# Loads of keys and values split between two DMA queues, in a one-token attention block

## The chip, the cores and the metric

The kernel runs on one core of a Trainium2 chip. The core has five engines that run their own instruction streams: TensorE (PE, matrix products), VectorE (DVE), ScalarE (ACT), GpSimd (POOL) and SyncE (SP), which here does nothing but issue DMAs. Sixteen DMA engines move data from the device memory into the on-chip memory of 128 partitions. An engine that issues a DMA puts it on its own DMA queue; SP's queue is q1 in the profile, ScalarE's is q10. Engines wait for one another, and for DMAs, on semaphores.

The metric is the device time of one execution in microseconds (us), the median of several runs. All times below are microseconds from the start of the profiled span unless something else is said.

## The reference

One token goes through a transformer block: layer norm, attention against a long cache, a projection with a residual, then a second layer norm and a small dense block. What counts is the attention, with 32 heads, 32,768 cached positions and a head size of 128, in bfloat16:

```
q = (layernorm(x) @ wq)                      # 512 -> 32 heads x 128
scores = einsum("bhqd,bhkd->bhqk", q, k_cache) * (Dh ** -0.5)
p = softmax(scores)
o = einsum("bhqk,bhkd->bhqd", p, v_cache)
h = x + o @ wo
out = h + (act(layernorm(h) @ w1 + b1)) @ w2     # 512 -> 1376 -> 512
```

The keys of one head are 32,768 x 128 x 2 bytes = 8.39 MB, and so are its values. Over 32 heads that makes 537 MB to read for one token; the weights add some 11 MB. Each byte is used once.

## The kernel before, in words

**Loads.** One head's keys (or values) are loaded as 128 rows of 64 KB, one for each partition: partition p gets positions 256 p to 256 p + 255. So a head is 256 "tiles" of 128 x 128 in on-chip memory, and tile r holds position 256 p + r of every p. There is room for the keys of two heads (even and odd heads have a place each) and the values of one. The places lie in `ring`, which has six slots of 128 tiles.

**Order of the loads.** `order` is a list made ahead: WQ, K0, then K1, V0, K2, V1, K3, V2 and so on (K2: keys of head 2), then WO, V31 and the weights of the dense block. SP walks through it in `program` and issues each load after the wait that makes its place free: keys of head h wait until the keys of head h - 2 have all been transposed, values of head h until the values product of head h - 1 is through. All loads are on SP's queue, one behind the other. `pieces` says into which pieces a load is cut, each piece with a semaphore of its own: K0 at tiles 64 and 192, K1 and V1 at 128, K31 at 64, V31 at 128, 192, 224 and 240. The rest are whole. `cut_sems` holds the semaphores of later pieces; where a load is not cut, `uncut` and `later_k` let SP add to these semaphores itself, so that the waits stay regular.

**The work on a head.** `k_group` (L673) takes eight tiles of keys, transposes them on TensorE into PSUM (L690), and VectorE copies them out (L696). TensorE then multiplies them by the query, one column of scores a tile (`scores`, L666), three groups later. After 256 tiles there are 32,768 scores in `S_ps`. `soft_max`, `soft_a` and `soft_b` find the greatest score over all partitions; `soft_exp` (L746, ScalarE) writes the exponentials into `pbuf`; `soft_c` sums them. `pv` (L717) multiplies the 256 tiles of values by them.

**The order of the engines.** In `rounds`, round i does `head(i)`: keys of head i, and then `rest(i)`: the values product of head i - 1, with the maximum of head i put between its parts, and last exp(i), which waits for that product since both use `pbuf`. TensorE and VectorE run the middle rounds as loops, so their waits are computed from the counter of the round: `_loop_waits` (L70) has a special case for "keys_in", the wait of the first tile of a head, which has one semaphore for each place of keys. ScalarE and SP have their instructions written out. ScalarE's only work in a middle round is exp; the only DMA it issues is the token itself, at the start.

On TensorE one round is thus: transposes and scores of head i, then 256 products of the values of head i - 1; and with the end of these products SP's wait for V(i) ends, and just behind it that for K(i + 2).

Of the kernel before, what the change touches and what calls it, by code (L numbers as in the profile page):

```python
# [13 lines left out]
PE, ACT, DVE, POOL, SP = "pe", "act", "dve", "pool", "sp"  # L14
# [4 lines left out]
def _name(key):  # L19
    return key if isinstance(key, str) else id(key)  # L20


class _Sched:
# [46 lines left out]
    def _loop_waits(self, eng, at):  # L70
        e = self.engines[eng]
        log = self.log[eng]
        first = min(n for n in log if at in log[n])
        rows = [log[n][at] for n in sorted(log) if at in log[n]]
        for ws in zip(*rows, strict=True):
            if ws[0] == "keys_in":

                for home, n in enumerate((self.counter >> 1, (self.counter + 1) >> 1)):
                    e.wait_ge(self._handle(self.sems["keys_in"][home]), n * 16 + 16)
                continue  # L80
            got = [self._resolve(w) for w in ws]
            key = got[0][0]
            vals = [v for _, v in got]
            step = vals[1] - vals[0]
            assert all(_name(k) == _name(key) for k, _ in got), ws
            assert all(v == vals[0] + step * n for n, v in enumerate(vals)), vals
            if step == 0:
                assert self.waited.get(_name(key), 0) >= vals[0], ws
                continue
            had = self.loop_waited.get(_name(key))  # L90
            if had is not None and had[1] == step and had[0] >= vals[0]:
                continue
            self.loop_waited[_name(key)] = (vals[0], step)
            base = vals[0] - step * first
            val = self.counter if step == 1 else self.counter * step
            e.wait_ge(self._handle(key), val + base if base else val)
# [211 lines left out]
def build_kernel(nc, A_x, A_k_cache, A_v_cache, A_wq, A_wo, B_w1, B_b1, B_w2, out):  # L308
# [3 lines left out]
    H = HD // Dh  # L312
# [9 lines left out]
    TPS = 128  # L322
    SLOT = TPS * Dh
    HALVES = Sk // (128 * TPS)
    SCOLS = HALVES * TPS
# [82 lines left out]
    sem = nc.alloc_semaphore  # L408
    kinds = [PE, ACT, DVE, POOL, SP, "exp", "pmax", "gmax", "qc", "nb", "rcp", "oev", "A", "B", "C", "qkh", "pv"] + [f"pv{r}" for r in V_EVENTS]
    kinds += [f"{k}{i}" for k in ("ev", "tr") for i in range(2 * GPS)]  # L410
    sems = {k: sem(f"s_{k}") for k in kinds}
    ready = [sem(f"ready{i}") for i in range(NS)]
    sems["keys_in"] = (ready[0], ready[HALVES])
    s_x = sem("s_x")
    s_b1 = sem("s_b1")
    s_out = sem("s_out")
# [8 lines left out]

    CUTS = {"k": [64, 192], "v": [TPS, 192, 224, 240]}

    def pieces(what):
        kind, h = what
        if what in (("k", 0), ("v", H - 1)):  # L430
            at = CUTS[kind]
        else:
            at = [TPS] if what in (("k", 1), ("v", 1)) else [64] if what == ("k", H - 1) else []
        return list(zip([0] + at, at + [SCOLS]))

    def cut_at(kind, h, r):
# [23 lines left out]
    cut_sems = {k: {r: sem(f"cut_{k}_{r}") for r in CUTS[k]} for k in CUTS}  # L460
# [40 lines left out]
    def tiles_of(what):  # L501
        return ring[:, slot_of(what):slot_of(what) + HALVES, :].rearrange("p s (r d) -> p (s r) d", d=Dh)

    def keys_of(cache, h):
        return cache[0, h, :, :].rearrange("(p r) d -> p r d", r=SCOLS)
# [16 lines left out]
    def done_with(kind, h, r0, r1):  # L522
        if kind == "v":
            return [f"pv{h}_{r1}" if r1 in V_EVENTS else f"pv{h}"]
        return [free_name(("k", h, half)) for half in range(HALVES) if r0 < (half + 1) * TPS and r1 > half * TPS]
# [1 line left out]
    events = {}  # L527

    def key_tile(S, at):
        if at in [0] + CUTS["k"]:  # L530
            key_addresses(S, at)
        off = S.home + at * Dh * 2
        return ring8[:, bass.ds(off, Dh * 2)].bitcast(BF16)
# [7 lines left out]
    def program(S):  # L541
        S.home_bytes = HALVES * SLOT * 2
        t_ = nc.tensor
        a = nc.scalar
        v = nc.vector
        g = nc.gpsimd
        sp = nc.sync


        def start(dst, src, s):  # L550
            S.dma(SP, lambda: sp.dma_start(dst, src).then_inc(s, 16))  # L551

        S.stay(DVE)
        S.dma(SP, lambda: sp.sem_inc(ready[HALVES], 16))
        for what in order:
            slot = slot_of(what)
            if what == ("k", 1):
                S.stay(SP)
            S.wait(SP, freed_by(what))
            flat = ring[:, slot, :]  # L560
            if what[0] == "wq":
                S.wait(SP, ["b1z"])
                start(b1r[0:FJ // 2, :], B_b1[0:FJ * 128].rearrange("(i p) -> i p", i=FJ // 2), s_b1)
                start(b1r[FJ // 2:FJ // 2 + 1, 0:FLAST], B_b1[FJ * 128:F].rearrange("(o p) -> o p", o=1), s_b1)
            elif what[0] == "wo":
                start(flat, A_wo.rearrange("(p j) n -> p (j n)", j=32), ready[slot])
            elif what == WL:
                start(wol_v[Dh - WB:Dh, :], A_wo[H * Dh - WB:H * Dh, :], s_wl)
            elif what[0] == "w1":
                k = what[1]  # L570
                start(w1_v[:, k, :], B_w1[k * 128:(k + 1) * 128, :], w1_sems[k])
            elif what[0] == "w2":
                n = what[1]
                if n + 1 < len(W2_J):
                    j0, j1 = W2_J[n], W2_J[n + 1]
                    start(w2_v[:, j0:j1, :].rearrange("p (i s) n -> p i (s n)", s=2),
                          B_w2[j0 * 128:j1 * 128, :].rearrange("(i p s) n -> p i (s n)", p=128, s=2), w2_sems[n])
                else:
                    start(w2_v[0:FLAST, FJ, :], B_w2[FJ * 128:F, :], w2_sems[n])
            else:  # L580
                kind, h = what
                rows = keys_of(A_k_cache if kind == "k" else A_v_cache, h)
                for r0, r1 in pieces(what):
                    if kind == "v" and h:
                        S.wait(SP, done_with(kind, h - 1, r0, r1))
                    if what == ("k", 1):
                        s = ready[slot] if r0 else s_k1
                    else:
                        s = cut_sems[kind][r0] if r0 else ready[slot]
                    start(tiles_of(what)[:, r0:r1, :], rows[:, r0:r1, :], s)  # L590


                for r, n in uncut(what) if kind == "v" else later_k(h):
                    S.dma(SP, lambda r=r, n=n: sp.sem_inc(cut_sems[kind][r], 16 * n))
        S.dma(SP, lambda: sp.dma_start(out[0, 0, :].rearrange("(c m) -> c m", c=KC), outr[0:128:32, :]).then_inc(s_out, 16),
              waits=["fin"])
# [45 lines left out]
        for h in range(H):  # L642
            for kc in range(KC):
# [4 lines left out]
                       waits=(["xn0", ready_wait(("wq",))] if h == 0 and kc == 0 else ()))  # L648
# [24 lines left out]
        def k_group(h, half, gi):  # L673
            what = ("k", h)
            bg = count[0]
            count[0] += 1
            tb = T_b[bg % NT]
            for r in range(GT):
                at = half * TPS + gi * GT + r
                waits = []  # L680
                if r == 0:
                    if at == 0:
                        waits.append("keys_in")
                    waits.append("identb")
                if at in CUTS["k"]:
                    waits.append((cut_sems["k"][at], 16 * (h + 1)))
                names = []
                if r == GT - 1:
                    names = [f"trb{bg}"] + ([free_name(what + (half,))] if gi == GPS - 1 else [])
                S.step(PE, lambda r=r, at=at: t_.matmul(tb[:, r * 128:(r + 1) * 128], key_tile(S, at), identb[:, :],  # L690
                                                        is_transpose=True, start=True, stop=True),
                       name=(names or None), waits=waits, kind=f"tr{bg % (2 * GPS)}")
            after = half * TPS + (gi + 1) * GT
            if after < SCOLS and after not in CUTS["k"]:
                key_addresses(S, after)
            S.step(DVE, lambda: v.tensor_copy(ering[:, bg % NE, :, :].rearrange("p r d -> p (r d)"), tb[:, :]),  # L696
                   name=f"ev{bg}", waits=[f"trb{bg}"],
                   kind=f"ev{bg % (2 * GPS)}")
            pend.append((h, half * TPS + gi * GT, bg))
            flush(KEEP)  # L700
# [39 lines left out]
        def soft_b(h):  # L740
            S.step(PE, lambda: t_.matmul(B_REG, onesm[0:1, :], gmax[:, :], start=True, stop=True),  # L741
                   name=f"B{h}", waits=[f"gmax{h}", "consts0"] + ([] if h else [(s_k1, 16)]), kind="B")
            S.step(DVE, lambda: v.tensor_scalar_mul(nb[:, :], B_REG, -SC), name=f"nb{h}", waits=[f"B{h}"], kind="nb")  # L743

        def soft_exp(h):
            S.step(ACT, lambda: a.activation(pbuf[:, :], S_ps[:, 0:SCOLS], ACTF.Exp,  # L746
                                             bias=nb[:, :], scale=SC, accum_out=esum[:, :]),
                   name=f"exp{h}", waits=[f"nb{h}"] + ([f"pv{h - 1}"] if h >= 1 else []), kind="exp")
# [173 lines left out]
```

## Time and profile before

| what | value |
|---|---|
| median of 3 runs | 1275.08 us (1275.01 to 1275.23) |
| profiled execution, first to last instruction (span) | 1273.1 us |
| bytes read | 548.09 MB, 431 GB/s over the span |
| DMA engines occupied by packets of SP's queue | 99.7% of the span |
| TensorE products busy / weight loads busy | 80% / 78% |
| VectorE busy | 56% |
| ScalarE busy | 2% |

Of the profiled execution the trace has the span; the time outside it, 2.0 us against the median of the runs, is what lies before the first and after the last recorded instruction. "Time to landing" of a load runs from its issue to the last count of its semaphore, so it includes the time that it stands behind earlier loads of its queue. The chain of waits is followed backward from the last instruction, at each step to what released it. "issue" is time in which an engine waited for nothing that the profile shows.

### The profile page before, as it was taken

Reading aid. Unit: us, or ns where it says so; the run is one execution under the profiler, and the core shown is the slowest. Engines: PE = TensorE matmul, PEld = TensorE weight load, DVE = VectorE, ACT = ScalarE, POOL = GpSimd, SP = SyncE. Lnnn points to the kernel's source line nnn. Section 1 sums busy time; section 2 is a strip of 40 time slices with the busy share of each in tenths; the row PEclk is TensorE's granted clock in tenths of the full one; section 3 lists DMA queues with packets and bytes.
Section 4 is the critical chain, followed back from the end, with each engine's and each line's share of the span. In section 5 each row is a group of like instructions: output and inputs, shape, how many; then the busy total and the mean of one; then the engine's idle time right before and its main releaser. Section 6 shows DMA issues by size and latency. Waiting matters only on the chain.

```text
span 1273.1 us, 54451 instructions
## 1 busy us (share of the span) xinstructions
PE 1019.9 (80%) x25046; PEld 993.3 (78%) x25047; DVE 718.2 (56%) x1257; ACT 20.6 (2%) x71; POOL 0.9 (0%) x7
## 2 busy tenths in 40 slices
PE   4789877779777789777798777797777897777996
PEld 4789877779777779777788777797777887777994
DVE  3656664456654456644566544566545666444661
ACT  0000000000000000000000000000000000000000
POOL 0000000000000000000000000000000000000000
PEclk9778877678877778776788777788767887777885
DMA  9999999999999999999999999999999999999998
GB/s 406 442 417 438 432 439 432 432 434 430 432 441 428 437 434 428 432 439 432 434 434 430 430 439 434 430 434 434 428 434 441 428 437 432 430 432 439 427 427 360
DMA packets 12214, 548.22 MB, mean 431 GB/s; under 512 B 1348, under 2 KB 1454, under 8 KB 2862
## 3 DMA queue, kind: packets, MB, share of 16 engines
q1 hardware_dynamic: 12204, 548.09, 99.7%
q8 instruction: 8, 0.13, 0.0%
q10 hardware_dynamic: 2, 0.00, 0.0%
HBM read 548.09 MB, written 0.00 MB: 431 GB/s over the span
## 4 chain that ended last, share of the span: by engine, by line
DMA 54%; DVE 23%; PE 19%; issue 2%; SPq 2%; POOL 0%; POOLq 0%
DMA ring<-in_A_k_cache_dram 51%; DVE ering L696 23%; PE ops L717 9%; PE tps L690 7%; DMA ring<-in_A_v_cache_dram 2%; SPq L551 2%; PE sps L666 1%; DMA ring<-in_B_w_dram 1%; PE hlp L741 1%; PE hlp L736 1%; PE hlp L751 0%; PE tps L867 0%; DVE pmax L730 0%; DVE perm L872 0%; DVE gmax L738 0%
## 5 line engine op out<-in xcount | busy, mean ns | idle before, releaser
L690 PE MATMUL tps<-identb,ring 128*128 128x128 bf16 x8192 | 671.7, 233 | 208.8 <-DMA ring<-in_A_k_cache_dram 203.2
L696 DVE COPY ering<-tps 128x1024 bf16<-128x1024 bf16 x1024 | 669.7, 691 | 261.6 <-PE tps L690 261.1
L690 PEld LDWEIGHTS tps<-identb,ring 128*128 x8192 | 525.4, 105 | 211.6 <-issue 211.6
L666 PE MATMUL sps<-qcur,ering 128*128 128x1 bf16 x8192 | 343.7, 164 | 7.3 <-DVE ering L696 6.6
L666 PEld LDWEIGHTS sps<-qcur,ering 128*128 128x128 bf16 x8192 | 309.4, 97 | 10.1 <-DVE ering L696 9.4
L717 PEld LDWEIGHTS ops<-pbuf,ring 128*128 128x128 bf16 x8192 | 226.4, 103 | 23.3 <-issue 15.1
L717 PE MATMUL ops<-pbuf,ring 128*128 128x1 bf16 x8192 | 231.3, 165 | 10.6 <-DMA ring<-in_A_v_cache_dram 7.2
L725 DVE TENSOR_TENSOR oT<-ops,rtotc 128x1 f32 x31 | 5.0, 161 | 110.6 <-PE ops L717 110.6
L738 DVE TENSOR_REDUCE gmax<-hlp 1x1 f32<-1x128 f32 x32 | 8.9, 279 | 64.5 <-PE hlp L736 64.5
L743 DVE TENSOR_SCALAR nbias<-hlp 128x1 f32<-128x1 f32 x32 | 5.1, 158 | 63.5 <-PE hlp L741 63.5
L746 ACT ACTIVATE pbuf<-sps,nbias 128x256 bf16<-128x256 f32 x32 | 15.2, 474 | 1219.7 <-PE ops L717 1166.8
L730 DVE TENSOR_REDUCE pmax<-sps 128x1 f32<-128x256 f32 x32 | 13.6, 424 | 14.3 <-PE sps L666 14.3
L736 PE MATMUL hlp<-ident,pmax 128*1 128x128 f32 x64 | 17.1, 363 | 2.5 <-issue 2.5
L741 PE MATMUL hlp<-gmax,onesmat 1*128 1x1 f32 x64 | 18.5, 356 | 0.4 <-DVE gmax L738 0.4
L741 PEld LDWEIGHTS hlp<-gmax,onesmat 1*128 1x128 f32 x64 | 15.8, 304 | 1.3 <-DVE gmax L738 0.9
L751 PE MATMUL hlp<-esum,onesmat 128*128 128x1 f32 x64 | 12.1, 259 | 4.7 <-issue 0.6
L751 PEld LDWEIGHTS hlp<-esum,onesmat 128*128 128x128 f32 x64 | 9.8, 191 | 7.1 <-issue 7.1
L645 PE MATMUL hlp<-xnT,ring 128*128 128x1 bf16 x128 | 3.6, 165 | 9.2 <-DMA ring<-in_A_wq_dram 9.2
L645 PEld LDWEIGHTS hlp<-xnT,ring 128*128 128x128 bf16 x128 | 3.5, 104 | 9.3 <-issue 9.3
L725 DVE TENSOR_TENSOR oL<-ops,rtotc 128x1 bf16<-128x1 f32 x1 | 0.2, 161 | 12.4 <-PE ops L717 12.4
L649 DVE CAST qT<-hlp 128x32 bf16<-128x32 f32 x1 | 0.2, 192 | 11.5 <-PE hlp L645 11.5
L746 ACT ACTIVATION_READ_ACCUMULATOR pbuf<-sps,nbias 128x1 f32 x32 | 6.2, 193 | 0.0
(82 smaller groups left out, 45.5 us busy)
## 6 DMA issues: line engine op xcount, KB each, us to landing
ring<-in_A_k_cache_dram SPq DMA_DIRECT2D x3, 4096.0 KB, 40.0
ring<-in_A_v_cache_dram SPq DMA_DIRECT2D x3, 4096.0 KB, 16.0
ring<-in_A_k_cache_dram SPq DMA_DIRECT2D x3, 2048.0 KB, 30.9
ring<-in_A_k_cache_dram SPq DMA_DIRECT2D x1, 6144.0 KB, 45.2
ring<-in_A_wq_dram SPq DMA_DIRECT2D x1, 4096.0 KB, 12.3
ring<-in_A_wo_dram SPq DMA_DIRECT2D x1, 4096.0 KB, 35.1
ring<-in_A_v_cache_dram SPq DMA_DIRECT2D x1, 2048.0 KB, 16.1
ring<-in_B_w_dram SPq DMA_DIRECT2D x4, 344.0 KB, 20.5
```

The lines of the kernel that those rows point to most:

```text
L551: S.dma(SP, lambda: sp.dma_start(dst, src).then_inc(s, 16))
L645: S.step(PE, lambda h=h, kc=kc: t_.matmul(Q_REG[:, h:h + 1], wq_v[:, kc, h * Dh:(h + 1) * Dh], xnT[:, 0, kc:kc + 1], start=(kc == 0), stop ...
L666: S.step(PE, lambda r=r: t_.matmul(S_ps[:, col0 + r:col0 + r + 1], ering[:, bg % NE, r, :], qcur[:, :], start=True, stop=True), name=(name ...
L690: S.step(PE, lambda r=r, at=at: t_.matmul(tb[:, r * 128:(r + 1) * 128], key_tile(S, at), identb[:, :], is_transpose=True, start=True, stop ...
L696: S.step(DVE, lambda: v.tensor_copy(ering[:, bg % NE, :, :].rearrange("p r d -> p (r d)"), tb[:, :]), name=f"ev{bg}", waits=[f"trb{bg}"], ...
L717: S.step(PE, lambda r=r: t_.matmul(o_ps[:, 0:1], vt[:, r, :], pbuf[:, r:r + 1], start=(r == 0), stop=(r == SCOLS - 1)), name=(names or Non ...
L730: S.step(DVE, lambda: v.tensor_reduce(pmax[:, :], S_ps[:, 0:SCOLS], AXX, ALU.max), name=f"pmax{h}", waits=[f"qkh{h}"], kind="pmax")
L736: S.step(PE, lambda: t_.matmul(A_REG, pmax[:, :], ident[:, :], start=True, stop=True), name=f"A{h}", waits=[f"pmax{h}", "ident", f"rcp{h - ...
L738: S.step(DVE, lambda: v.tensor_reduce(gmax[:, :], A_REG, AXX, ALU.max), name=f"gmax{h}", waits=[f"A{h}"], kind="gmax")
L741: S.step(PE, lambda: t_.matmul(B_REG, onesm[0:1, :], gmax[:, :], start=True, stop=True), name=f"B{h}", waits=[f"gmax{h}", "consts0"] + ([] ...
L746: S.step(ACT, lambda: a.activation(pbuf[:, :], S_ps[:, 0:SCOLS], ACTF.Exp, bias=nb[:, :], scale=SC, accum_out=esum[:, :]), name=f"exp{h}", ...
L751: S.step(PE, lambda: t_.matmul(C_REG, onesm[:, :], esum[:, :], start=True, stop=True), name=f"C{h}", waits=[f"exp{h}"], kind="C")
```

## The change

The loads of K2 to K30 and of V2 to V29, 57 in all, are each cut at tile 128. SP issues the first 128 tiles, ScalarE the other 128 on its own queue. K0, K1, K31, V0, V1, V30, V31 and the weights stay with SP as they were.

For values of head h both issues wait until the values product of head h - 1 is through. For keys of head h + 2 SP's issue waits until all keys of head h have been transposed, and ScalarE's until the last of them has. On ScalarE the two issues stand in `soft_exp(h)`, ahead of exp(h): first the values of head h, then the keys of head h + 2. On SP the order of `order` stays.

TensorE waits for the second half at tile 128 of a head's keys, on a pair of new semaphores ("keys_mid", one for each place), as it does for the first at tile 0; for values, the wait at tile 128 that was there already now has a DMA of its own behind it. The addresses of the group of tiles at 128 are now written behind that wait (`key_tile`) and no longer at the end of the group before it.

```diff
@@ _loop_waits
-            if ws[0] == "keys_in":
+            if ws[0] in ("keys_in", "keys_mid"):
                 for home, n in enumerate((self.counter >> 1, (self.counter + 1) >> 1)):
-                    e.wait_ge(self._handle(self.sems["keys_in"][home]), n * 16 + 16)
+                    e.wait_ge(self._handle(self.sems[ws[0]][home]), n * 16 + 16)
...
+    sems["keys_mid"] = (sem("mid0"), sem("mid1"))
...
+    def by_two(what):
+        return what[0] in ("k", "v") and 2 <= what[1] <= (H - 2 if what[0] == "k" else H - 3)
@@ pieces
+        elif what in (("k", 1), ("v", 1)) or by_two(what):
+            at = [TPS]
@@ key_tile
-        if at in [0] + CUTS["k"]:
+        if at in [0, 64, TPS, 192]:
             key_addresses(S, at)
@@ program, SP's part
+        S.dma(SP, lambda: sp.sem_inc(sems["keys_mid"][0], 16))
+        S.dma(SP, lambda: sp.sem_inc(sems["keys_mid"][1], 32))
...
                 for r0, r1 in pieces(what):
+                    if by_two(what) and r0:
+                        continue
                     if kind == "v" and h:
-                        S.wait(SP, done_with(kind, h - 1, r0, r1))
+                        S.wait(SP, done_with(kind, h - 1, r0, SCOLS if by_two(what) else r1))
@@ k_group
                     if at == 0:
                         waits.append("keys_in")
+                    if at == TPS:
+                        waits.append("keys_mid")
...
-            if after < SCOLS and after not in CUTS["k"]:
+            if after < SCOLS and after not in (64, TPS, 192):
                 key_addresses(S, after)
@@ before soft_exp
+        def second_half(what, waits):
+            kind, h = what
+            if by_two(what):
+                S.dma(ACT, lambda: a.dma_start(tiles_of(what)[:, TPS:SCOLS, :],
+                                               keys_of(A_k_cache if kind == "k" else A_v_cache, h)[:, TPS:SCOLS, :])
+                      .then_inc(cut_sems["v"][TPS] if kind == "v" else sems["keys_mid"][h % 2], 16), waits=waits)
+
         def soft_exp(h):
+            second_half(("v", h), [f"pv{h - 1}"])
+            second_half(("k", h + 2), done_with("k", h, TPS, SCOLS))
             S.step(ACT, lambda: a.activation(pbuf[:, :], S_ps[:, 0:SCOLS], ACTF.Exp,
```

More of the change, by code (lines that the diff above doesn't have):

```diff
@@ L426, in build_kernel @@
     CUTS = {"k": [64, 192], "v": [TPS, 192, 224, 240]}
+    def by_two(what):
+        return what[0] in ("k", "v") and 2 <= what[1] <= (H - 2 if what[0] == "k" else H - 3)
     def pieces(what):
-        kind, h = what
-        if what in (("k", 0), ("v", H - 1)):
-            at = CUTS[kind]
+        if what == ("k", 0):
+            at = [64, 192]
+        elif what == ("v", H - 1):
+            at = CUTS["v"]
+        elif what in (("k", 1), ("v", 1)) or by_two(what):
+            at = [TPS]
         else:
-            at = [TPS] if what in (("k", 1), ("v", 1)) else [64] if what == ("k", H - 1) else []
+            at = [64] if what == ("k", H - 1) else []
         return list(zip([0] + at, at + [SCOLS]))
@@ L565, in program @@
             elif what[0] == "wo":
+                S.dma(SP, lambda: sp.sem_inc(sems["keys_mid"][1], 16))
                 start(flat, A_wo.rearrange("(p j) n -> p (j n)", j=32), ready[slot])
```

## The prediction

> **What bounds the kernel now.** I read the DMA part of the page first, then who waits for whom, then the chain of waits in order of time.
>
> ```profile
> span 1273.1 us, 54451 instructions
> DMA  9999999999999999999999999999999999999998
> q1 hardware_dynamic: 12204, 548.09, 99.7%
> q8 instruction: 8, 0.13, 0.0%
> DMA 54%; DVE 23%; PE 19%; issue 2%; SPq 2%; POOL 0%; POOLq 0%
> PE tps L690 <- DMA ring<-in_A_k_cache_dram: 203.2, 30, 7.8
> ```
>
> One queue, q1 (SP's), keeps the 16 DMA engines occupied for 99.7% of the span, and TensorE waits 30 times, 6.8 us each, for keys to land. The bytes are the bound. So the only questions are whether the bytes flow at another rate with two queues, and whether the engines run dry anywhere. The chain shows the rhythm:
>
> ```profile
> 126.47 42.94 DMA ring<-in_A_k_cache_dram
> 169.42 0.40 issue
> 169.82 3.59 PE tps L690 x32
> 201.99 44.83 DMA ring<-in_A_k_cache_dram
> 247.29 3.59 PE tps L690 x32
> ```
>
> K4 (keys of head 4) lands at 169.4 and K6 at 246.8: two heads, 33.55 MB, in 77.4 us, that is 38.7 us a head, 19.35 us for one load of 8.39 MB and 9.68 us for half of one. Nothing can be gained but rate.
>
> Now the issues on SP's queue, and the times to landing of V0, K2, V1 (two pieces) and K3, one row each in that order, then WQ's, the very first load (issued at 0.75):
>
> ```profile
> 16.71 0.33 SPq L551 DMA_DIRECT2D ring<-in_A_v_cache_dram  x1
> 52.52 0.33 SPq L551 DMA_DIRECT2D ring<-in_A_k_cache_dram  x1
> 85.69 7.86 SPq L551 DMA_DIRECT2D ring<-in_A_v_cache_dram  x2
> 93.22 0.33 SPq L551 DMA_DIRECT2D ring<-in_A_v_cache_dram  x1
> 93.65 0.36 SPq L551 DMA_DIRECT2D ring<-in_A_k_cache_dram  x1
> 125.98 0.33 SPq L551 DMA_DIRECT2D ring<-in_A_v_cache_dram  x1
> 201.55 0.33 SPq L551 DMA_DIRECT2D ring<-in_A_v_cache_dram  x1
> ...
> ring<-in_A_v_cache_dram SPq DMA_DIRECT2D x1, 55.9
> ring<-in_A_k_cache_dram SPq DMA_DIRECT2D x1, 39.4
> ring<-in_A_v_cache_dram SPq DMA_DIRECT2D x1, 4096.0 KB, 16.0
> ring<-in_A_v_cache_dram SPq DMA_DIRECT2D x1, 4096.0 KB, 18.2
> ring<-in_A_k_cache_dram SPq DMA_DIRECT2D x1, 37.1
> ring<-in_A_wq_dram SPq DMA_DIRECT2D x1, 4096.0 KB, 12.3
> ```
>
> V0 lands at 72.6 (so K1, just ahead of it, at 53.25), K2 at 91.9, V1's pieces at 101.7 and 111.4, K3 at 130.75. The next issue, at 125.98 when the values product pv(1) ends, comes 4.8 us before the queue would be empty. **That backlog is what protects the bound**; later it is larger (issue at 201.55, K5 lands 38.7 after K4, at 208.1: 6.6 us).
>
> **The change, part by part.**
>
> *The rate.* Each of 57 loads (28 of values, 29 of keys) now goes as two times 128 rows of 32 KB, not 128 rows of 64 KB. K1, cut at 128, already has 32 KB rows and V0 64 KB rows:
>
> ```profile
> 33.00:53.00 20.00, 16.10 (x348) 15.79 (x346) 13.84 (x22) 0.00 (x0) 0.00 (x0) 0.84 1.02 436
> 55.00:72.00 17.00, 14.76 (x291) 14.18 (x292) 12.58 (x21) 0.56 (x2) 0.00 (x0) 0.80 1.00 433
> 169.41:1200.00 1030.59, 834.83 (x20640) 817.16 (x20641) 597.54 (x1022) 14.70 (x52) 0.00 (x0) 0.77 1.00 433
> ```
>
> 436 and 433 GB/s (last column) differ by no more than what packets begun in a short window make. From K2's landing to K3's, with V1 in halves, 38.85 us pass against 38.7. Bounds for a cut: 0 to 0.1 us, 0 to 5.7 us over 57. I take 0.4 us in all, near the lower end. No row shows two queues both full; engines busy 1.00 leave no gain to fill, and 433 against 436 bounds one at 0.7%, 7 us, of which I take nothing.
>
> *Issues and waits on ScalarE.* Two issues of 0.33 us stand ahead of each exp. Both wait for events that exp or an earlier step waits for anyhow, so exp comes some 0.8 us later. Behind exp wait C(h) and the next head's first scores, and ahead of these lie the 6.8 us for keys; with that cover gone there are still the 32 transposes of 3.59 us (row at 169.82). Cost nothing. TensorE gets a wait before tile 128 and writes its addresses behind it; nearest is the 0.81 us of issue that the head loop has ahead of its transposes. It too lies in the 6.8 us; where they are gone it costs 0 to 0.8, of which I take 0.
>
> *The order of the bytes in the first heads.* Here the change does more than halve. K2's and K3's second halves are issued on ScalarE as soon as keys of head 0 and 1 are transposed, past everything that stands ahead on SP's queue:
>
> ```profile
> 51.41 1.01 PE L690 MATMUL tps<-identb,ring 128*128 128x128 bf16 x8
> 79.40 0.61 PE L690 MATMUL tps<-identb,ring 128*128 128x128 bf16 x8
> 81.53 1.81 PE L717 MATMUL ops<-pbuf,ring 128*128 128x1 bf16 x64
> 94.00 3.59 PE L690 MATMUL tps<-identb,ring 128*128 128x128 bf16 x32 [0.81 <-issue]
> 57.84 0.47 ACT L746 ACTIVATE pbuf<-sps,nbias 128x256 bf16<-128x256 f32 x1 [52.94 <-DVE nbias L743]
> ```
>
> Keys of head 0 are through at 52.4 and those of head 1 at 80.0; ScalarE is idle at 52.4, and from 58.5 on. So K2's second half is issued at 52.5, K3's at 80.0. The latter was behind V1 before, issued at 93.65 and begun at 111.4. Does a second queue get served while the first is full? The trace has one such queue, q8, which brings instructions while K0 and K1 are queued on q1 up to 53.25:
>
> ```profile
> 45.49 3.23 issue
> 86.55 3.35 issue
> ```
>
> TensorE sits for 3.2 to 3.4 us without a cause that the profile shows and goes on, with q1 full for longer both times; I read that as an instruction fetch that was served within those 3.4 us, not behind q1's backlog. So I take equal sharing. With it, ahead of the end of K2's first half stand V0, all of K2, and K3's second half: 53.25 + 19.35 + 19.35 + 9.68 = 101.6. If engines alternate row by row, K2's first half ends about a row before that, 100.4 (9.68 / 8 rows an engine = 1.2). I take 101.0, against 91.9 before. V0, sharing with K2's second half, lands at 81 to 83.6, so pv(0) starts up to 2.5 us late (81.53 to 84.0), which hides in the wait for K2.
>
> Keys of head 2 then start at 101.0 + 0.4 = 101.4, not 94.0. From there to the end of pv(1) took 125.98 - 94.0 = 31.98; V1 lands by 101.6 + 19.35 = 121, ahead of its use at some 125. So pv(1) ends at **133.4**. All bytes up to K3 are unchanged in sum and K3 still lands at 130.75. What follows is issued only at 133.4: **the engines run dry**, 2.65 us, and restart. WQ took 12.3 for 9.68 us of bytes: a start costs 0 to 2.6 us, I take 1.7, nearer the measured end. Loss: 2.65 + 1.7 = 4.35 us, bounds 2.05 + 0 and 3.2 + 2.6 + 0.8 = 2.1 to 6.6.
>
> *After that.* Both queues restart empty and get equal halves at one moment. Head 3 runs 133.4 to 166 (0.8 + 31.98), K4 lands 4.35 late at 173.8, backlog 7.6 us; from then on the old rhythm. Heads 30 and 31 stay on SP with V30, so the end only shifts.
>
> **Sum.** 1273.1 + 4.35 + 0.4 = 1277.9 us of span. The median of the runs is 2.0 above the span (time outside first to last instruction, taken as unchanged): **1279.8 us**, its own range 1277.5 to 1284.
>
> **The rivals.**
>
> *No dry spell (not slower).* If an engine takes a whole load's rows in turn, or goes by the order of issue, K2's first half is not behind K3's second. It decides by whether pv(1) ends before 129.8 (130.75 less about 1 to restart), so whether K2's first half lands before 97.4. With V0, K2's second half, K2's first half in turn: 53.25 + 38.7 = 92.0, pv(1) ends where it did, time 1275.1 + 0.4 = 1275.5. For it: no row shows two large queues. Against it: the two gaps of 3.3 us, short beside the 19.35 us of a whole load. The Trainium skill, "DMA: Bandwidth & Descriptors", section "Queues, rings and completion order", speaks for it: it has each engine go round its queues by packets of typically 9 to 17 descriptors before it switches. Eight rows of a load and its semaphore write would be about such a packet, by which the time would be 1275.5; the 3.2 us gap at 45.49 sits badly with turns that long.
>
> *Unequal sharing, dry again and again (much slower).* If SP's half got 40%: from an empty start, 31.1 us of the 38.7 queued are moved when a head (32.8) ends; 6.9 of SP's are left, at 0.4 they take 17.2, and the next head ends 17.2 + 31.4 = 48.6 later, with 46.3 queued: 2.3 + 1.7 = 4.0 us dry every other head, 14 times 4.0 = 56, plus 4.7: 1336 us. At 45% it is 11.9 + 31.4 = 43.3, under 46.3: nothing. The point is near 43%. Nothing in the trace speaks for such a bias.
>
> *Two full queues move more.* At the 0.7% above, 7 us on 1030, less 4.7: 1272.8. Busy 1.00 with one queue speaks against it.
>
> **How the numbers follow.** Dry spell 0.65; no dry spell 0.23; unequal sharing, or a price of switching rows that the trace can't show, 0.08; more rate 0.04. About 0.2%, 2.5 us, can be told from no change: 1272.5 to 1277.6 is the same. The lowest part of the first case (dry of 2.1, 1277.5) adds 0.04 to the second: faster 0.03, same 0.28, slower 0.69. Range: from the no-spell case, 1275.0, to the dry spell's upper bound with a dear cut, 1284.8.
>
> **What would show it.** Right: TensorE's start on head 2 goes from 94.0 to about 101; a slice with DMA under 9 near 131 to 135; ScalarE's queue with 57 halves, some 239 MB; then 38.7 us a head and 433 GB/s as before. K3's second half landing before K2's first would show the sharing. Wrong: head 2 at 94 (the queues take turns by loads); DMA busy without a gap at 131 but a later end (the cut costs rate); gaps at every other head (unequal sharing); waits of TensorE before tile 128 in the middle heads (ScalarE's half arrives late).

## The result, and the profile after

The changed kernel takes 1284.46 us (1284.03 to 1284.92, 4 runs) against 1275.15 for the kernel before, measured on the same chip: a ratio of 1.0073, 95% interval 1.0059 to 1.0087. It is slower by 9.3 us; 4.7 had been forecast, with 1284.8 as the upper end of the range.

The page of the profile after, in the lines that answer to those shown of before:

```profile
span 1283.1 us, 54514 instructions
DMA  9999899999999999999999999999999999999998
GB/s 402 433 429 433 364 428 433 433 425 440 426 437 429 431 434 426 439 427 434 432 430 434 427 437 429 432 432 430 435 428 434 431 433 432 427 435 430 438 428 351
q1 hardware_dynamic: 12204, 309.02, 56.2%
q10 hardware_dynamic: 8210, 239.08, 43.3%
DMA 58%; DVE 21%; PE 17%; SPq 2%; issue 1%
```

ScalarE's queue carries the 239 MB, and the two queues share the 16 engines. One slice of the 40, the fifth, moves 364 GB/s. It holds the time from 128 to 160 us. The stretches around the forecast gap (columns: stretch, its length, busy time of PE, its weight loads, DVE, ACT and POOL, granted clock, DMA share, GB/s):

```profile
128.00:130.00 2.00, 2.00 (x61) 1.97 (x59) 0.16 (x1) 0.00 (x0) 0.00 (x0) 0.50 0.42 180
130.75:133.90 3.15, 2.38 (x85) 2.30 (x83) 0.16 (x1) 0.04 (x1) 0.00 (x0) 0.50 0.00 0
134.00:136.50 2.50, 2.50 (x26) 2.50 (x25) 1.40 (x3) 0.43 (x2) 0.00 (x0) 0.50 0.99 354
```

For 3.15 us nothing moves, the engines tail off before that (0.42), and after the restart the first rows are slow (354 GB/s with engines occupied 0.99). The chain of waits shows why, and what the later heads cost:

```profile
101.19 3.59 PE tps L704 x32
132.97 0.33 SPq L558
133.40 40.87 DMA ring<-in_A_k_cache_dram
...
206.30 45.84 DMA ring<-in_A_k_cache_dram
...
1139.94 44.96 DMA ring<-in_A_k_cache_dram
```

Head 2 starts at 101.19, pv(1) ends at 132.97, and only then are V2 and K4 issued. K4 lands at 174.27, 4.86 us later than before. From its landing to that of K30, at 1184.90, 1010.63 us pass for 26 heads. Before the change K30 landed at 1175.70 (this row is of the kernel before):

```profile
1130.65 45.05 DMA ring<-in_A_k_cache_dram
```

From K4, at 169.41, that was 1006.29. So the later heads lose another 4.34 us, 0.33 for two heads or **0.08 us a load**, and 4.86 + 4.34 = 9.2 us is what K30 comes late, nearly all of the 9.3 between the medians. In this profiled execution, the slowest of the four, the result itself is issued 10.0 us later than before (1281.08 against 1271.07). The last 0.8 us fall behind K30, and no run here explains them. K6 lands at 252.14, so two heads take (1184.90 - 252.14) / 12 = 77.73 us, against 77.41.

### The profile page after: what moved, and what is told of

Its sections match the earlier page's. It is cut to its first block, busy times and chain, and to the rows that moved or that the text cites. A ratio compares the mean times of both kernels' runs of the same rounds, so it can differ in the third digit from the quotient of the medians.

```text
span 1283.1 us, 54514 instructions
## 1 busy us (share of the span) xinstructions
PE 1018.6 (79%) x25046; PEld 991.8 (77%) x25047; DVE 718.1 (56%) x1257; ACT 20.6 (2%) x71; POOL 0.9 (0%) x7
## 4 chain that ended last, share of the span: by engine, by line
DMA 58%; DVE 21%; PE 17%; SPq 2%; issue 1%
DMA ring<-in_A_k_cache_dram 55%; DVE ering L710 21%; PE ops L731 9%; PE tps L704 6%; DMA ring<-in_A_v_cache_dram 2%; SPq L558 2%; DMA ring<-in_B_w_dram 1%; PE sps L678 1%; PE hlp L755 1%; PE hlp L750 1%; PE hlp L774 0%; PE tps L890 0%; SPq L905 0%; DVE perm L895 0%; SPq L68 0%
```

## The experiments

### Both halves on one queue

The same cuts and waits, but SP issues both halves.

```diff
                 for r0, r1 in pieces(what):
-                    if by_two(what) and r0:
-                        continue
...
+                    elif by_two(what) and r0 and kind == "k":
+                        s = sems["keys_mid"][h % 2]
...
         def soft_exp(h):
-            second_half(("v", h), [f"pv{h - 1}"])
-            second_half(("k", h + 2), done_with("k", h, TPS, SCOLS))
```

> Both halves of each of the 57 loads stay cut at tile 128 with the same waits on TensorE, but SP issues them one behind the other on its own queue; ScalarE issues none. Theory A (what costs a steady head 0.16 us is that rows of two queues take turns): two heads take 77.41 to 77.45 us as before the change, no dry spell, 1275.2 to 1276.0 us. Theory B (rows of 32 KB cost more than rows of 64 KB, on one queue as on two): two heads take 77.7 us, 1279.5 to 1280.0 us. Either way head 2 starts at 94 and the engines do not run dry at 131.

1282.13 us (5 runs), ratio 1.0055, interval 1.0042 to 1.0068. The chain of this run, two landings of values two heads apart, the issue of the result, and the span:

```profile
270.95 34.85 DMA ring<-in_A_v_cache_dram
348.68 34.85 DMA ring<-in_A_v_cache_dram
...
1275.71 0.61 SPq L607 DMA_DIRECT2D out_dram<-perm  x1
span 1280.1 us, 54542 instructions
```

305.80 to 383.53 is 77.73 us: the full excess of the changed kernel, with one queue. Theory B holds: **the rows of 32 KB cost it, not the second queue.** The result is issued at 1275.71, 4.6 us later than before (1271.07), which is that excess; 2.4 us more lie between that issue and the end (1280.1 - 1275.71 = 4.4 against 2.0), where this build has a packet of instructions on another queue. That part is put down to the build's layout by its place alone and has not been tried further; it made the total miss the 1280.0 of theory B.

### K3's second half held back

```diff
-            second_half(("k", h + 2), done_with("k", h, TPS, SCOLS))
+            second_half(("k", h + 2), done_with("k", h, TPS, SCOLS) + ([f"pv{h - 1}"] if h else []))
```

> One wait is added to the changed kernel: ScalarE's issue of the second half of K3 waits also for the values product of head 0, so that it no longer stands ahead of K2's first half. Theory of the dry spell: head 2 starts at 94 again, no gap of the DMA engines near 131 to 134, and the changed kernel's 1284.5 loses 4.7 us: 1279.8. By turns row by row K3's first half then runs alone on SP's queue when values 2 and keys 4 are issued, so the starts of the heads should alternate, some 41 and 36 us apart, without a gap. Rival (the loss up to K4 is the slower rate or something else in the first heads): within 1 us of 1284.5.

1279.57 us (5 runs), ratio 1.0034, interval 1.0021 to 1.0047: 4.9 us less than the changed kernel. The stretch of the gap and the start of head 2 in this run:

```profile
130.75:133.90 3.15, 0.10 (x2) 0.11 (x3) 0.00 (x0) 0.00 (x0) 0.00 (x0) 0.50 0.99 427
92.95 3.59 PE L704 MATMUL tps<-identb,ring 128*128 128x128 bf16 x32 [0.81 <-DMA ring<-in_A_k_cache_dram]
125.05 0.33 SPq L558 DMA_DIRECT2D ring<-in_A_v_cache_dram  x1
165.44 0.33 SPq L558 DMA_DIRECT2D ring<-in_A_v_cache_dram  x1
203.01 0.33 SPq L558 DMA_DIRECT2D ring<-in_A_v_cache_dram  x1
241.31 0.33 SPq L558 DMA_DIRECT2D ring<-in_A_v_cache_dram  x1
```

The gap is gone, and with it 4.9 of the 9.3 us. One issue held by one wait was the whole difference, so **the early issue of K3's second half is the cause of the dry spell**. The alternation came only once: issues 40.4, 37.6 and 38.3 us apart. The expectation that it would go on was wrong; why it settles was not worked out.

### Only K2 and K3 split

`by_two` holds for K2 and K3 alone; all other loads are whole, on SP, which adds to "keys_mid" itself for the keys that are no longer cut.

```diff
-        return what[0] in ("k", "v") and 2 <= what[1] <= (H - 2 if what[0] == "k" else H - 3)
+        return what in (("k", 2), ("k", 3))
```

> Only K2 and K3 are split between the queues; all later loads are whole and SP's, as before the change. Theory of the dry spell as a loss of its own: the gap near 131 to 134 is there, K4 lands some 4.8 us later than before the change, and from then on two heads take 77.41 us: 1275.1 + 4.8 = 1279.9. Rival (the loss needs the later halves on two queues): under 1277.

1280.88 us (1278.39 to 1281.73, 5 runs), ratio 1.0040, interval 1.0027 to 1.0053. The gap, and two rows of the chain for the rhythm after it:

```profile
130.95:134.90 3.95, 3.11 (x115) 3.03 (x112) 0.16 (x1) 0.56 (x2) 0.00 (x0) 0.50 0.00 0
208.02 44.56 DMA ring<-in_A_k_cache_dram
1136.84 44.68 DMA ring<-in_A_k_cache_dram
```

Two split loads of the first heads alone make it 5.7 us slower, with 1181.52 - 252.58 = 928.94 us over 24 heads, 77.41 for two. So the dry spell is a loss of its own. It is less steady than the rate: the runs lie 3.3 us apart, and these rows are of the slowest of them.

### Split by partitions, 0 to 63 and 64 to 127

```diff
-                S.dma(ACT, lambda: a.dma_start(tiles_of(what)[:, TPS:SCOLS, :],
+                S.dma(ACT, lambda: a.dma_start(tiles_of(what)[64:128, :, :],
...
-                    start(tiles_of(what)[:, r0:r1, :], rows[:, r0:r1, :], s)
+                    if by_two(what):
+                        start(tiles_of(what)[0:64, :, :], rows[0:64, :, :], s)
```

> The 57 loads are split between the queues by partitions and not by tiles: SP issues partitions 0 to 63, ScalarE 64 to 127, so all rows are 64 KB as before the change and an engine changes queue 8 times a load and not 16 times. TensorE waits for both halves at tile 0, for values too; V31's first piece is 192 tiles. If each turn costs (about 5 ns), two heads take 77.57 us, half of the excess of 0.32, and the total is 1284.5 - 2.3 = 1282.2 us. If two busy queues cost by the byte, 77.73 us and 1284.5. If the rows of 32 KB cost, 77.41 us and 1280. The dry spell near 131 stays in all three.

2390.51 us (2213.95 to 2468.05, 6 runs): none of the three. A stretch in its middle:

```profile
600.00:1800.00 1200.00, 500.16 (x12264) 487.30 (x12262) 354.55 (x607) 8.48 (x30) 0.00 (x0) 0.64 1.00 218
```

The engines are occupied throughout and move half as much, 218 GB/s. As a test of what turns between queues cost it says nothing, but it raised a question of its own, which the next runs answer.

### The same two halves on one queue, and the split by even and odd partitions

First both halves of 64 neighbouring partitions on SP:

```diff
+                        p0 = 64 if r0 else 0
+                        start(tiles_of(what)[p0:p0 + 64, :, :], rows[p0:p0 + 64, :, :], s)
```

> The loads in halves of 64 neighbouring partitions (0 to 63, then 64 to 127), both on SP's queue, none on ScalarE's. If the half rate belongs to the 64 neighbouring partitions, about 217 GB/s and 2400 us again. If it took two queues, 433 GB/s and 1275 to 1277 us.

2478.34 us (2 runs), ratio 1.944, interval 1.940 to 1.947:

```profile
600.00:1800.00 1200.00, 462.18 (x11377) 450.46 (x11374) 322.80 (x556) 8.48 (x30) 0.00 (x0) 0.62 1.00 208
```

So it is the 64 neighbouring partitions and not the queues. The Trainium skill, "SBUF — State Buffer", section "Door 1: The DMA port swizzle (why `[64,N]` ≈ `[32,N]`)", has it that the rate goes by how many of 16 ports the partitions reach, and that partitions 0 to 63 reach eight. By that rule half of 433 GB/s, 217, is the estimate for one such load, and the trace agrees with 208 here.

Why did two queues that cover both halves between them not help? The packets of the run with two queues, a row each, point to a reason in two stretches, one behind the other, 600 to 604.84 and 604.84 to 609.68 us, each about as long as one row takes (queue, packets, MB, share of the 16 engines):

```profile
q1 hardware_dynamic: 14, 0.92, 87.3%
q10 hardware_dynamic: 2, 0.13, 12.4%
...
q10 hardware_dynamic: 14, 0.92, 87.3%
q1 hardware_dynamic: 2, 0.13, 12.5%
```

Most engines take a row of SP's queue together and then one of ScalarE's, so most of the time nearly all of them write to the same 64 partitions. They are not always so much in step: in a stretch as long from 1500 us on it is 10 of 16. This fits the half rate; no run keeps the turns out of step to try it.

Then SP takes the even partitions and ScalarE the odd ones, in whole rows of 64 KB:

```diff
-                        start(tiles_of(what)[0:64, :, :], rows[0:64, :, :], s)
+                        start(tiles_of(what)[0:128:2, :, :], rows[0:128:2, :, :], s)
...
-                S.dma(ACT, lambda: a.dma_start(tiles_of(what)[64:128, :, :],
+                S.dma(ACT, lambda: a.dma_start(tiles_of(what)[1:128:2, :, :],
```

> Split by partitions again, but SP takes the even ones and ScalarE the odd ones, so that each half reaches over all 128 partitions; rows of 64 KB, two queues. Theory A (a fixed price of some 9 ns for each row, nothing for two queues): two heads take 77.41 us as before the change, the dry spell stays, 1275.1 + 5 = 1280. Theory B (splitting by partitions halves the rate because two queues disturb each other): about 2400 us again. Theory C (half the rate came from the 64 neighbouring partitions): as A.

1283.21 us (1280.40 to 1283.65, 4 runs), ratio 1.0064, interval 1.0048 to 1.0081. Theory B is ruled out, but the median is 3.2 above the 1280 of the other two. The profiled execution is the fastest of the four, so its rows below show less than the median lost; what sets the other three apart is open. The same with K3's second half held back:

> The split by even and odd partitions, and K3's second half held back until the values product of head 0, as in the run that took the dry spell away. If rows and dry spell are all that the change costs, two heads take 77.41 us, no gap near 131, and the time is that before the change: 1275.1 to 1275.8. If two queues cost something of their own, 1277 or more.

1278.89 us (7 runs), ratio 1.0030, interval 1.0019 to 1.0042. First the gap and two landings of the run without the hold, then two landings and the gap's place of the run with it:

```profile
130.40:132.10 1.70, 0.81 (x22) 0.73 (x20) 0.16 (x1) 0.00 (x0) 0.00 (x0) 0.50 0.00 0
204.41 45.85 DMA ring<-in_A_k_cache_dram
437.96 44.59 DMA ring<-in_A_k_cache_dram
```

```profile
203.92 44.88 DMA ring<-in_A_k_cache_dram
436.11 44.97 DMA ring<-in_A_k_cache_dram
129.00:131.00 2.00, 0.66 (x25) 0.58 (x22) 0.16 (x1) 0.00 (x0) 0.00 (x0) 0.50 0.39 131
1274.96 0.61 SPq L610 DMA_DIRECT2D out_dram<-perm  x1
```

(482.55 - 250.26) / 3 and (481.08 - 248.80) / 3 are both 77.43 us for two heads: with 64 KB rows **two full queues cost 0.02 us**, next to nothing, and the second DMA of each load, with its semaphore write, is in it. The stretch without any transfer goes with the hold again, and 4.3 us of the median with it.

The time, 1278.89, is above the expected 1275.8 and also above 1277, which by the expectation would say that two queues cost something of their own. In the steady heads they do not; the loss comes at two other places. K6 lands 1.98 us late (246.82 before). K3's second half now takes turns with V1, whose second piece lands at 121.4 (111.4 before), and this experiment waits for all of V1 at tile 0:

```profile
121.49 1.84 PE L733 MATMUL ops<-pbuf,ring 128*128 128x1 bf16 x64 [4.19 <-DMA ring<-in_A_v_cache_dram]
```

So pv(1) ends late, at 129.69, and the engines nearly run dry at 129 to 131. And the result is issued at 1274.96, 3.9 late: 1.9 more come behind K6, most of them at the end, where V31's first piece is 192 tiles. The wait at tile 0 and the longer first piece are this experiment's own; V1's late landing comes of the two queues. No run takes these parts one by one.

### Shorter rows still

One queue as in the first experiment, with the second half cut once more, at tile 192.

```diff
+                    for q0, q1 in ([(TPS, 192), (192, SCOLS)] if by_two(what) and r0 else [(r0, r1)]):
+                        start(tiles_of(what)[:, q0:q1, :], rows[:, q0:q1, :], s)
```

> All on SP's queue; the first half of each of the 57 loads in rows of 32 KB, the second half cut once more, at tile 192, in rows of 16 KB: 24 rows an engine and load, not 16. A fixed price of a row (two heads took 77.41 us with 32 rows an engine and 77.73 with 64, so 10 ns a row) puts two heads at 77.73 + 32 x 0.010 = 78.05 us; if rows below 64 KB had one price whatever their length, 77.73 us.

1284.95 us (4 runs), ratio 1.0076, interval 1.0059 to 1.0093.

```profile
272.59 34.53 DMA ring<-in_A_v_cache_dram
350.63 34.51 DMA ring<-in_A_v_cache_dram
```

385.14 - 307.12 = 78.02 us for two heads, 78.05 expected. Per engine, two heads go as 32, 64 and 96 rows and take 77.41, 77.73 and 78.02 us: each row more costs 10 and then 9 ns, though the second step adds rows of 16 KB and the first rows of 32 KB. Each step also adds one DMA a load; by the even and odd split that makes up 0.02 us of it, which leaves 9.4 and 8.4 ns a row. At 0.15 us a load the 57 loads make 8.7 of the 9.9 us that this run is slower.

### exp ahead of the issues

From head 2 on, ScalarE's two issues stand behind exp.

```diff
         def soft_exp(h):
-            second_half(("v", h), [f"pv{h - 1}"])
-            second_half(("k", h + 2), done_with("k", h, TPS, SCOLS))
+            if h < 2:
+                second_half(("k", h + 2), done_with("k", h, TPS, SCOLS))
             S.step(ACT, lambda: a.activation(pbuf[:, :], ...
+            if h >= 2:
+                second_half(("v", h), [f"pv{h - 1}"])
+                second_half(("k", h + 2), done_with("k", h, TPS, SCOLS))
```

> The changed kernel with exp put ahead of ScalarE's two issues from head 2 on, so that exp is no longer some 0.8 us late; ScalarE's halves are issued some 0.7 us later instead. If the issues ahead of exp cost nothing, as predicted, 1284.0 to 1284.9 as the changed kernel; if exp's delay was on the path in the steady heads, 28 times 0.8 is 22 us less; if the only cost is in the dry spell, where ScalarE's halves now start later, up to 0.7 us more.

1284.10 us (1283.48 to 1285.70, 4 runs), ratio 1.0073, interval 1.0056 to 1.0090: no different from the changed kernel. The 22 us of an exp on the path in every head are ruled out.

## Why the prediction was right and wrong

**The direction, the mechanism and the place were right.** Forecast: slower, by engines that run dry near 131 us because K3's second half overtakes. Held back, the loss goes (1279.57); alone, it stays (1280.88). The size was not: 4.7 us were forecast and 9.3 measured. That the time still lies in the range is in part luck: it is 0.3 us below the upper end, 1284.8, and that end is lower than what the upper bounds of the two terms give together (1275.1 + 6.6 + 5.7 = 1287.4).

**Its steps, one by one.** These are issues and times to landing of V0 (SP, issued 16.80 in this run), K2's two halves (ScalarE 51.59, SP 51.65), K3's second half (ScalarE 80.04) and K3's first (SP 92.86), after the change:

```profile
ring<-in_A_v_cache_dram SPq DMA_DIRECT2D x1, 65.8
ring<-in_A_k_cache_dram ACTq DMA_DIRECT2D x1, 4096.0 KB, 31.8
ring<-in_A_k_cache_dram SPq DMA_DIRECT2D x1, 4096.0 KB, 49.1
ring<-in_A_k_cache_dram ACTq DMA_DIRECT2D x1, 4096.0 KB, 24.4
ring<-in_A_k_cache_dram SPq DMA_DIRECT2D x1, 4096.0 KB, 38.3
```

K2's first half lands at 100.75 (forecast 101.0), pv(1) ends at 132.97 (133.4), K3 lands at 131.2 (130.75, as the queue moves the same bytes). V0, with eight rows of 64 KB an engine, and K2's second half, with eight of 32 KB, land together, at 82.6 and 83.4; shares equal in bytes would have put the latter at 72.6. The packets on the two queues from 56 to 80 us agree: as many on the one as on the other, and nearly twice the bytes on V0's.

```profile
q1 hardware_dynamic: 111, 6.59, 63.4%
q10 hardware_dynamic: 112, 3.67, 35.6%
```

So the turns go **row by row**. That settles the rival in which a whole load goes at once. It went by the Trainium skill's packets of 9 to 17 descriptors ("DMA: Bandwidth & Descriptors", section "Queues, rings and completion order"): here a turn is a single row, and the measurement decides against it.

One sign that the prediction named did not come: K3's second half landed at 104.4, behind K2's first and not before it. The sum that gave 101.6 had all of it ahead; by turns row by row, for which the prediction had 100.4, a part of it comes behind. The reading of TensorE's two gaps of 3.3 us as fetches that did not wait behind q1 pointed the right way. In the run before, one packet of q8 lies in each of them (45.4 to 48.8 and 86.5 to 90 us), which fits; that TensorE waited for it is not shown.

**The price of the dry spell** came out at 4.9 us by the run with the hold, 4.3 between the two runs with even and odd partitions, 5.7 in the run of K2 and K3 alone; forecast 4.35 (bounds 2.1 to 6.6). The wait for pv(1) was 1.8 us behind K3's landing, not 2.65, and the restart cost more than 1.7. Of the 4.86 us by which K4 is late, four split loads ahead of it make 0.3 and the wait 1.8, so about 2.7 are left. The engines do not run out together (0.42 busy from 128 to 130), and the first rows after the restart are slow.

**The step that failed was the rate.** "I take 0.4 us in all, near the lower end": measured 57 times 0.08 = 4.6. The mechanism was named and the bound, 5.7, held it; the term was mis-sized more than tenfold. The trace had hinted at it: 38.85 us from K2's landing to K3's, with one load in halves, against 38.7, is an excess of 0.15 for one cut. These landings are given to 0.1 us, so the row is coarse, but it speaks for the upper bound and not for the lower. GB/s of two windows, 436 against 433, which could not resolve 0.4%, were given more weight than that difference. The sum with the measured terms is 4.9 + 4.6 = 9.5, against 9.3.

**At nothing, and rightly:** the issues ahead of exp; the sharing itself. No gap shows at every other head (77.73 us throughout, against the 1336 us of unequal sharing), and no rate was gained: two full queues with rows of 64 KB take 77.43 against 77.41 us. The 31.4 us for a head in the working of unequal sharing stands in no row (169.41 to 201.55, from K4's landing to the end of pv(3), is 32.1); nothing else hangs on it.

No version that beats the kernel before came out of the runs. The best of them with two queues, 1278.89, has neither short rows nor the early issue, and still loses 3.8 us in the first heads and at the end.

## What to carry to other kernels

When a transfer is split over two queues, draw each queue by itself for the first rounds: a half that is issued past what stood ahead of it takes its share of the engines from the piece that is needed first, and the loss shows rounds later, where nothing is left to move. Where bytes are the bound, count the rows: each costs a fixed time, here 8 to 10 ns, and a difference of 0.1 us between two landings, taken 57 times, weighs more than a rate in whole GB/s. If a load must be split, split it so that rows keep their length and each part reaches over all partitions, as the even and odd split does here; it kept the rate, though it won nothing.

## What the runs showed of the hardware that was not expected

A load to 64 neighbouring partitions moves at half the rate: 208 GB/s with both halves on one queue, 218 with the halves on two queues, whose engines mostly turn to the same half together. Halves of every second partition, side by side on two queues, keep the full 433. Each row costs 8 to 10 ns beside its bytes, between 16 and 64 KB. And two queues take turns by rows, so the one with the longer rows moves more bytes (6.59 against 3.67 MB in 24 us).
